# Loads of the first phase cut so that each writes 128 partitions, w1's bits issued from ScalarE's queue, and the first phase put in an order written by hand

## The chip, the core and the metric

The kernel runs on one core of a Trainium2 chip. The metric is the device time of one execution in microseconds (us). Before the change it is 899.99 us, the median of three runs (896.8 to 904.1). The profiled execution of the same kernel took 902.82 us, and its profile spans 901.0 us.

## What is computed

Packed attention, in which 32 packed queries per head first attend to the 576 tokens, and the tokens then attend to the 32 results. The output goes through a token mixer of rank 32 and a channel mixer with a relu. There are 8 batches, 8 heads of size 64, 512 channels and 2048 hidden channels.

```
p_packed = softmax(p @ k.T / 8) @ v          # 32 x 64 per head
x        = softmax(q @ p_packed.T / 8) @ p_packed
h        = x.T @ U @ V                       # mixes tokens, rank 32
u        = x + h.T
out      = u + relu(u @ w_ch1) @ w_ch2
```

The inputs q, k, v and p are float32. U, V, w_ch1 and w_ch2 are float64 in memory, and the kernel reads their bits as pairs of int32 and makes float32 of them itself.

## The kernel before

**The first phase** works through 16 units, each of one batch and four heads. Per unit it loads k and v, turns k onto the other axis on TensorE (`a_turn`, tiles `kx`, `k_ps`, `kT`), makes scores (`a_scores`), takes their maximum and exponential (`a_softmax`), turns them back (`a_turn_back`, tiles `m_ps`, `eT`), multiplies with v (`a_pack`, tile `vt`) and turns the result into `ppT` (`a_heads`). A loop over `i` runs from 0 to 18. In pass `i` the scores belong to unit `i`, the turning of k to unit `i+1`, the load of k to `i+2` and of v to `i+1`, the product with v to `i-2`. Beside this the phase converts w1 from its float64 bits in 16 chunks (`load_w1`, `convert_w1`, tile `bits`), runs the token side of batch 0 (the list `first`), and loads the first q's (`load_nat` into tile `x`).

**The second phase** is a loop over 8 batches and 16 tiles `kt` of hidden channels. `gemm1` (tile `h_ps`, line 573) and `gemm2` (tile `o`, line 589) both run as three matmuls (`mm3`, lines 84 to 86). Between them stand the folding of w1 with the packed attention (`fold`), the token side of the next batch (`steps`), the conversion of w2 in the first batch, and the stores (line 604).

**What sets the order.** In the first phase a scheduler with a cost model places the instructions on the engines; in the second the order is that of the source (`manual_schedule`, line 524). Each engine runs its instructions in order and waits on semaphores. All DMAs are issued from SyncE's queue (SPq), in order. There are eight semaphores for DMAs, taken in turn over all queues, so a DMA also waits until the one eight before it has landed.

**The shapes of the DMAs** matter below. A DMA has a list of dimensions on the DRAM side and one on the SBUF side. k was loaded by one DMA of 128 x 2 x 576 on both sides (line 194). v goes by two DMAs of 64 x 4 x 256 to one half of the partitions each (line 394), and w1 by two of 64 x 1024 (line 137). Line 604 stores tokens 64 apart in two groups: its side in DRAM is 2 x 64 x 512 and its side in SBUF 128 x 512.

Of the kernel before, what the change touches and what calls it, by code (L numbers as in the profile page):

```python
# [8 lines left out]
F32 = mybir.dt.float32  # L9
F32R = mybir.dt.float32r  # L10
I32 = mybir.dt.int32
# [8 lines left out]
def packed_attention_mixer_kernel(  # L20
# [26 lines left out]
    nc = tc.nc  # L47
    B, H, S, D = q.shape
# [4 lines left out]
    P = 128  # L53
    SM = 512
    NT = 9
    I = S // NT
    NK = DF // P
    NU = 2 * B
    QW = 512
# [4 lines left out]
    LAST = slice(4 * I, 5 * I)  # L64
# [3 lines left out]
    U, V, w1, w2 = (a.bitcast(I32) for a in (U, V, w1, w2))  # L68
# [24 lines left out]
    def bank():  # L93
        return psT.tile([P, 512], F32, name="t_ps", tag="t")
# [8 lines left out]
    def ppT_tile():  # L103
        return pipe.tile([P, 2, P], F32, name="ppT", bufs=3)
# [21 lines left out]
    def bits_tile():  # L126
        return pipe.tile([P, 512, 2], I32, name="bits", bufs=2)

    chunks = [(x, c) for c in range(NPC) for x in range(4)]
    bits = {}  # L130

    def load_w1(n):
        x, c = chunks[n]
        b = bits["w1", n] = bits_tile()
        for g in range(2):
            r0 = 4 * D * g + D * x
            nc.sync.dma_start(out=b[64 * g:64 * g + 64].rearrange("p x t -> p (x t)"),
                              in_=w1[r0:r0 + D, 2 * QW * c:2 * QW * c + 2 * QW])

    def convert_w1(n):  # L140
        x, c = chunks[n]
        float32_of(conv_tile(I32), conv_tile(F32), bits.pop(("w1", n)), w1t[x][:, QW * c:QW * c + QW])
# [48 lines left out]


    def load_nat(x, src, b, g):
        nc.sync.dma_start(
            out=x.rearrange("p (h y) -> p h y", h=2),
            in_=src[b, 4 * g:4 * g + 4].rearrange("(h z) (i c) d -> (z i) h (c d)", z=2, c=NT))

    def turn(t, x, h, bank):

        x = x.rearrange("p (h y) -> p h y", h=2)  # L200
        t_ps = bank()
        if h < 2:
            for j in range(4):
                o = P * (2 * (j % 2) + j // 2)
                nc.tensor.transpose(t_ps[:, o:o + P], x[:, h, P * j:P * j + P], ident)  # L205
            nc.scalar.copy(t[:, 2 * h:2 * h + 2, :4 * I].rearrange("p z (j i) -> p j z i", j=4),
                           t_ps.rearrange("p (j z i) -> p j z i", j=4, z=2))
        else:
            for h in range(2):
                nc.tensor.transpose(t_ps[:64, P * h:P * h + P], x[:, h, SM:], ident)  # L210
            nc.scalar.copy(t[:64, :, LAST], t_ps[:64, :2 * P].rearrange("p (h i) -> p h i", h=4))

    def scores(lT, t, g, bank):

        ss = [bank() for _ in range(2)]
        for h in range(4):
            hs = slice(32 * h, 32 * h + 32)
            for r in range(2):
                rs = slice(64 * r, 64 * r + 64)
                n = HALF[r].stop - HALF[r].start  # L220
                nc.tensor.matmul(ss[r][hs, :n], lhsT=lT[rs, g, hs], rhs=t[rs, h, :n], start=True, stop=True)  # L221
        return [ss[r][:, :HALF[r].stop - HALF[r].start] for r in range(2)]
# [142 lines left out]


    actx = ExitStack()
    sA = actx.enter_context(tc.tile_pool(name="sA", bufs=2, reuse_waits="tile"))
    psA = actx.enter_context(tc.tile_pool(name="psA", bufs=2, space=PSUM, reuse_waits="tile"))

    UN = [(b, g) for b in range(B) for g in range(2)]
    ua = {}
    pn, pT, pps = {}, {}, {}

    def bank_a(tag):
        return lambda: psA.tile([P, 512], F32, name=f"{tag}_ps", tag=tag)

    def a_load(u):
        b, g = UN[u]
        ua[u] = {}  # L380
        if g == 0:
            pn[b] = sA.tile([P, 2, 2, D], F32, name="pn")
            for z in range(2):
                nc.sync.dma_start(out=pn[b][:, :, z], in_=p[b].rearrange("(g h) n d -> (h n) g d", g=2))
        ua[u]["x"] = sA.tile([P, 2 * S], F32, name="kx", bufs=3)
        load_nat(ua[u]["x"], k, b, g)

    def a_load_v(u):
        b, g = UN[u]
        vt = ua[u]["v"] = sA.tile([P, 5, 4 * D], F32, name="vt", bufs=3)  # L390
        rows = v[b, 4 * g:4 * g + 4].rearrange("h (i c) d -> i c h d", c=NT)
        main = v[b, 4 * g:4 * g + 4].rearrange("h (i c) d -> i h (c d)", c=NT)[:, :, :8 * D]
        for a in range(2):
            nc.sync.dma_start(out=vt[64 * a:64 * a + 64, :4], in_=main[:, :, 4 * D * a:4 * D * a + 4 * D])
        nc.sync.dma_start(out=vt[:64, 4].rearrange("p (h d) -> p h d", h=4), in_=rows[:, 8])

    def a_p(b):
# [6 lines left out]
    def a_turn(u):  # L404
        b, g = UN[u]
        if g == 0:
            a_p(b)
        ua[u]["t"] = sA.tile([P, 4, 5 * I], F32, name="kT")
        for h in range(3):
            turn(ua[u]["t"], ua[u]["x"], h, bank_a("k"))  # L410

    def a_scores(u):
        b, g = UN[u]
        ua[u]["s"] = scores(pT[b], ua[u]["t"], g, bank_a("s"))

    def a_softmax(u):
        ss = ua[u]["s"]
        mx = sA.tile([P, 3], F32, name="mx")
        sm = ua[u]["sum"] = sA.tile([P, 2], F32, name="sm", bufs=3)
        for r in range(2):  # L420
            nc.vector.tensor_reduce(mx[:, r:r + 1], ss[r], axis=AX.X, op=ALU.max, negate=True)
        nc.vector.tensor_tensor(mx[:, 2:], mx[:, :1], mx[:, 1:2], op=ALU.min)
        e1 = ua[u]["e"] = sA.tile([P, S], F32, name="e1")
        for r in range(2):
            nc.scalar.activation(e1[:, HALF[r]], ss[r], AF.Exp, bias=mx[:, 2:], accum_out=sm[:, r:r + 1])
# [15 lines left out]
    def a_pack(u):  # L441
        b, g = UN[u]
        eT, vt = ua[u]["eT"], ua[u]["v"]
        p_ps = bank_a("m")()
        vk = vt[:, :4].rearrange("p h x -> p (h x)").rearrange("p (h k d) -> p k h d", h=4, k=4)
        for kk in range(5):
            rows = P if kk < 4 else I
            for h in range(4):
                hs = slice(32 * h, 32 * h + 32)
                rhs = vk[:, kk, h] if kk < 4 else vt[:rows, 4, D * h:D * h + D]  # L450
                nc.tensor.matmul(p_ps[hs, :D], lhsT=eT[:rows, kk, hs], rhs=rhs, start=kk == 0, stop=kk == 4)
        two = ua[u]["two"] = sA.tile([P, 2, D], F32, name="two")
        nc.scalar.activation(two, p_ps[:, :D].unsqueeze(1).to_broadcast([P, 2, D]), AF.Copy, scale=ua[u]["rs"])
        nc.gpsimd.tensor_copy(ppall[:, b, g], two[:, 0])

    def a_heads(u):
        b, g = UN[u]
        if g == 0:
            pps[b] = ppT_tile() if b == 0 else sA.tile([P, 2, P], F32, name="ppTa")
        z_ps = bank()  # L460
        nc.tensor.transpose(z_ps[:, :P], ua[u]["two"].rearrange("p z d -> p (z d)"), ident)
        nc.scalar.copy(pps[b][:, g], z_ps[:, :P])  # L462
        if g == 1:
            if b == 0:
                ppT[0] = pps[0]
            else:
                nc.sync.dma_start(out=ppTd[b], in_=pps[b].rearrange("p g n -> p (g n)"))
# [1 line left out]
    a_load(0)  # L469
    a_load(1)  # L470
    a_load_v(0)
    load_w1(0)
    load_w1(1)
    a_turn(0)
    n_w1 = 0
    first = attention(0, res)

    def some_w1():
        nonlocal n_w1
        if n_w1 < 16:  # L480
            convert_w1(n_w1)
            if n_w1 + 2 < 16:
                load_w1(n_w1 + 2)
            n_w1 += 1

    for i in range(NU + 3):
        if 0 <= i - 1 < NU:
            a_turn_back(i - 1)
        if i < NU:
            a_scores(i)  # L490
        if i + 1 < NU:
            a_load_v(i + 1)
            a_turn(i + 1)
        if i + 2 < NU:
            a_load(i + 2)
        some_w1()
        if i < NU:
            a_softmax(i)
        if i >= 5:
            for _ in range(2):  # L500
                if first:
                    first.pop(0)()
        if 0 <= i - 2 < NU:
            a_pack(i - 2)
        if 0 <= i - 3 < NU:
            a_heads(i - 3)
        if i == 2:
            uv = load_uv()
        if i == 3:
            prepare_uv(*uv)  # L510
        if i == 13:
            load_w2(0)
            load_w2(1)
        if i == 14:
            fold(0, 0)
        if i == 16:
            steps = attention(1, res)
            steps.pop(0)()
            split_w2(*convert_w2(0))
            load_w2(2)  # L520
    actx.close()


    ctx.enter_context(tc.manual_schedule())
    sB = ctx.enter_context(tc.tile_pool(name="sB", bufs=2, reuse_waits="tile"))
    psH = ctx.enter_context(tc.tile_pool(name="psH", bufs=1, space=PSUM, reuse_waits="tile"))
    psO = ctx.enter_context(tc.tile_pool(name="psO", bufs=4, space=PSUM, reuse_waits="tile"))
# [118 lines left out]
    for b in range(B):  # L646
# [3 lines left out]
        for kt in range(NK):  # L650
# [19 lines left out]
            if kt % 4 == 2 and (b, kt) != (B - 1, NK - 2):  # L670
                n = b * NPC + kt // 4 + 1
# [49 lines left out]
```

## Time and profile before

| what | value |
|---|---|
| median of three runs | 899.99 us |
| profiled execution: its own time, its span | 902.82 us, 901.0 us |
| TensorE (PE) busy | 842.1 us, 93% of the span |
| VectorE (DVE), ScalarE (ACT), GpSimd (POOL) busy | 379.4, 331.5, 93.9 us |
| DMA | 59.08 MB, mean 66 GB/s |
| chain that ended last | PE 80%, DMA 10%, DVE 5%, ACT 2% |

A share of busy time is a mean over both phases. The "DMA share" of a window is the mean busy share of the core's 16 DMA engines, so that one engine busy all the time is 0.0625. TensorE's granted clock is 1.00 in nearly all of the second phase.

### The profile page before, as it was taken

The page shows a single profiled execution, that of the slowest core. Times are in us where ns is not written, and L with a number is a line of the kernel's source. Part 1 is how long each engine was busy: PE and PEld are TensorE (multiplying, and loading weights), DVE is VectorE, ACT ScalarE, POOL GpSimd, SP SyncE. Part 2 cuts the span into 40 slices and gives each one's busy share as a digit, 9 for nine tenths or more (in the row PEclk, how much of TensorE's full clock was granted, in tenths as well). Part 3 has the DMA queues.
Part 4 walks back from the last instruction along what each step waited for, and adds up shares of the span by engine and source line. Part 5 has one row for each costly group of instructions (what it writes and reads, how often), then busy time and mean ns, then how long its engine had stood idle before and what let it go on. Part 6 is the DMA issues. An engine that isn't in the chain of part 4 may idle for free.

```text
span 901.0 us, 14507 instructions
## 1 busy us (share of the span) xinstructions
PE 842.1 (93%) x5808; PEld 670.3 (74%) x5808; DVE 379.4 (42%) x892; ACT 331.5 (37%) x952; POOL 93.9 (10%) x111
## 2 busy tenths in 40 slices
PE   5788983999999999999999999999999999999995
PEld 2454653877888887888888888788878887888884
DVE  2455666888534333333334323334343234332320
ACT  3565753544432333333323423234233332332220
POOL 0001122232201010011010101110111001000000
PEclk9787876999999999999999999999999999999998
DMA  9999985223110101001100110010001100000001
GB/s 223 243 255 233 243 202 147 93 95 108 47 45 1 59 11 49 1 1 59 42 6 2 59 59 1 1 59 29 19 1 59 39 21 1 1 17 32 1 3 57
DMA packets 38291, 59.08 MB, mean 66 GB/s; under 512 B 11088, under 2 KB 21200, under 8 KB 38224
## 3 DMA queue, kind: packets, MB, share of 16 engines
q1 hardware_dynamic: 38224, 58.16, 23.8%
q8 instruction: 46, 0.75, 0.4%
q14 instruction: 21, 0.17, 0.1%
HBM read 47.79 MB, written 10.35 MB: 65 GB/s over the span
## 4 chain that ended last, share of the span: by engine, by line
PE 80%; DMA 10%; DVE 5%; ACT 2%; issue 1%; SPq 1%; POOL 0%; DVEq 0%; ACTq 0%
PE o L84 15%; PE o L85 15%; PE o L86 15%; PE h_ps L84 8%; PE h_ps L86 7%; PE h_ps L85 7%; DMA bits<-in_moe_w_ch_dram 5%; PE t_ps L354 3%; DMA kx<-in_k_dram 2%; DMA vt<-in_v_dram 2%; PE t_ps L221 2%; PE t_ps L205 1%; DVE os L76 1%; PE t_ps L296 1%; DVE os L78 1%
## 5 line engine op out<-in xcount | busy, mean ns | idle before, releaser
L84 PE MATMUL o<-w2h,hh 128*128 128x512 f32 x512 | 207.2, 405 | 0.0
L85 PE MATMUL o<-w2l,hh 128*128 128x512 f32 x512 | 202.0, 395 | 0.0
L86 PE MATMUL o<-w2h,hl 128*128 128x512 f32 x512 | 201.8, 394 | 0.0
L580 DVE SCALAR_TENSOR_TENSOR hl<-h_ps,hh 128x256 fp32r<-128x256 f32 x256 | 104.2, 422 | 199.1 <-ACT hj L579 186.7
L84 PE MATMUL h_ps<-ah,wth 128*128 128x320 f32 (+1 forms) x512 | 159.4, 311 | 14.0 <-DVE hl L580 14.0
L577 ACT ACTIVATE hh<-h_ps 128x256 fp32r<-128x256 f32 x256 | 99.0, 388 | 193.0 <-PE h_ps L86 192.5
L85 PE MATMUL h_ps<-al,wth 128*128 128x320 f32 (+1 forms) x512 | 152.8, 298 | 0.0
L86 PE MATMUL h_ps<-ah,wtl 128*128 128x320 f32 (+1 forms) x512 | 152.5, 298 | 0.0
L84 PEld LDWEIGHTS h_ps<-ah,wth 128*128 128x128 f32 x512 | 98.0, 191 | 46.1 <-issue 25.7
L86 PEld LDWEIGHTS o<-w2h,hl 128*128 128x128 f32 x512 | 96.7, 189 | 22.2
L84 PEld LDWEIGHTS o<-w2h,hh 128*128 128x128 f32 x512 | 97.2, 190 | 21.4 <-issue 3.6
L85 PEld LDWEIGHTS o<-w2l,hh 128*128 128x128 f32 x512 | 97.4, 190 | 16.5
L85 PEld LDWEIGHTS h_ps<-al,wth 128*128 128x128 f32 x512 | 98.2, 192 | 1.9
L86 PEld LDWEIGHTS h_ps<-ah,wtl 128*128 128x128 f32 x512 | 98.1, 192 | 0.0
L361 DVE TENSOR_TENSOR wtl<-t_ps,wth 128x256 fp32r<-128x256 f32 x128 | 48.5, 420 | 94.3 <-ACT wth L360 91.0
L360 ACT CAST wth<-t_ps 128x256 fp32r<-128x256 f32 x128 | 43.3, 375 | 109.5 <-PE t_ps L354 98.5
L316 POOL TENSOR_TENSOR al<-aT,ah 128x320 fp32r<-128x320 f32 (+1 forms) x32 | 26.3, 823 | 207.1 <-ACT ah L315 207.0
L260 POOL TENSOR_TENSOR e<-e,m 128x576 f32<-128x576 f32 x16 | 18.7, 1170 | 240.4 <-DVE m L259 240.4
L76 DVE TENSOR_SCALAR os<-os 128x512 f32<-128x512 f32 (+2 forms) x35 | 21.0, 599 | 36.6 <-ACT os L75 36.6
L354 PE MATMUL t_ps<-w1t,ppT 64*32 64x512 f32 x512 | 35.9, 601 | 0.4 <-ACT ppTa L462 0.4
L205 PE MATMUL k_ps<-ident,kx 128*128 128x128 f32 x128 | 24.5, 344 | 11.5 <-DMA kx<-in_k_dram 8.5
L315 ACT CAST ah<-aT 128x320 fp32r<-128x320 f32 (+1 forms) x32 | 13.9, 434 | 53.0 <-DVE aT L314 53.0
(117 smaller groups left out, 1000.1 us busy)
## 6 DMA issues: line engine op xcount, KB each, us to landing
kx<-in_k_dram SPq DMA_DIRECT2D x16, 576.0 KB
x<-in_q_dram SPq DMA_DIRECT2D x16, 576.0 KB
vt<-in_v_dram SPq DMA_DIRECT2D x32, 256.0 KB
bits<-in_moe_w_ch_dram SPq DMA_DIRECT2D x32, 256.0 KB
bits<-in_moe_w_ch_dram SPq DMA_DIRECT2D x16, 512.0 KB
out_dram<-bits SPq DMA_DIRECT2D x32, 256.0 KB
pn<-in_p_dram SPq DMA_DIRECT2D x16, 64.0 KB
vt<-in_v_dram SPq DMA_DIRECT2D x16, 64.0 KB
```

The costliest lines, as they stand in the source:

```text
L76: nc.vector.tensor_single_scalar(t, t, LEAST, op=ALU.max)
L84: nc.tensor.matmul(ps, lhsT=lh, rhs=rh, start=start, stop=False)
L85: nc.tensor.matmul(ps, lhsT=lh, rhs=rl, start=False, stop=False)
L86: nc.tensor.matmul(ps, lhsT=ll, rhs=rh, start=False, stop=stop)
L205: nc.tensor.transpose(t_ps[:, o:o + P], x[:, h, P * j:P * j + P], ident)
L260: nc.gpsimd.tensor_tensor(e, e, m.unsqueeze(2).to_broadcast([P, S // 32, 32]), op=ALU.subtract)
L316: nc.gpsimd.tensor_tensor(al[:, g, ns], aT[:, ns], ah[:, g, ns].bitcast(F32), op=ALU.subtract)
L354: nc.tensor.matmul(f_ps[g][xs], lhsT=ppT[b][gs, g, xs], rhs=w1t[x][gs, QW * c:QW * c + QW], start=True, stop=True)
L360: nc.scalar.copy(hi[:, g], f_ps[g][:, cs])
L361: nc.vector.tensor_tensor(lo[:, g], f_ps[g][:, cs], hi[:, g].bitcast(F32), op=ALU.subtract)
L577: nc.scalar.activation(hh[:, ms], src, AF.Relu)
L580: nc.vector.scalar_tensor_tensor(hl[:, ms], src, 0.0, hh[:, ms].bitcast(F32), op0=ALU.max, op1=ALU.subtract)
```

## The change

The loads of k and q become two DMAs per unit instead of one, with the heads taken in another pairing (`turn` follows). v's main part becomes four DMAs per unit, one for each head, and each chunk of w1 one DMA instead of two, issued from ScalarE's queue and four chunks ahead instead of two. `a_softmax` is split into `a_max` and `a_exp`, the pass is written in another order, two chunks of w1 are converted in each of the passes 3 to 7, and `manual_schedule` begins before the first phase.

```diff
     def load_w1(n):
         x, c = chunks[n]
-        b = bits["w1", n] = bits_tile()
-        for g in range(2):
-            r0 = 4 * D * g + D * x
-            nc.sync.dma_start(out=b[64 * g:64 * g + 64].rearrange("p x t -> p (x t)"),
-                              in_=w1[r0:r0 + D, 2 * QW * c:2 * QW * c + 2 * QW])
+        b = bits["w1", n] = bits_tile() if n % 2 else sA.tile([P, 512, 2], I32, name="bits2")
+        nc.scalar.dma_start(out=b.rearrange("p x t -> p (x t)"),
+                            in_=w1.rearrange("(g x d) n -> x g d n", g=2, x=4)[x, :, :, 2 * QW * c:2 * QW * c + 2 * QW])
...
     def load_nat(x, src, b, g):
-        nc.sync.dma_start(
-            out=x.rearrange("p (h y) -> p h y", h=2),
-            in_=src[b, 4 * g:4 * g + 4].rearrange("(h z) (i c) d -> (z i) h (c d)", z=2, c=NT))
+        heads = src[b, 4 * g:4 * g + 4].rearrange("(z h) (i c) d -> h z i (c d)", z=2, c=NT)
+        for h in range(2):
+            nc.sync.dma_start(out=x[:, S * h:S * h + S], in_=heads[h])
...
-        main = v[b, 4 * g:4 * g + 4].rearrange("h (i c) d -> i h (c d)", c=NT)[:, :, :8 * D]
-        for a in range(2):
-            nc.sync.dma_start(out=vt[64 * a:64 * a + 64, :4], in_=main[:, :, 4 * D * a:4 * D * a + 4 * D])
+        main = v[b, 4 * g:4 * g + 4].rearrange("h (i c) d -> h i (c d)", c=NT)[:, :, :8 * D]
+        for h in range(4):
+            nc.sync.dma_start(out=vt[:, h], in_=main[h].rearrange("i (a x) -> a i x", a=2))
...
     actx = ExitStack()
+    ctx.enter_context(tc.manual_schedule())
...
     for i in range(NU + 3):
+        if i < NU:
+            a_scores(i)
+            a_max(i)
         if 0 <= i - 1 < NU:
             a_turn_back(i - 1)
-        if i < NU:
-            a_scores(i)
         if i + 1 < NU:
             a_load_v(i + 1)
             a_turn(i + 1)
         if i + 2 < NU:
             a_load(i + 2)
-        some_w1()
         if i < NU:
-            a_softmax(i)
+            a_exp(i)
+        if 0 <= i - 2 < NU:
+            a_pack(i - 2)
+        if 0 <= i - 3 < NU:
+            a_heads(i - 3)
+        for _ in range(2 if 2 < i < 8 else 1):
+            some_w1()
```

On the side of DRAM the new loads are 2 x 64 x 576 (k and q: the two heads `z`, 64 rows `i`), 2 x 64 x 256 (v: the two halves `a` of a row) and 2 x 64 x 1024 (w1: the two groups `g`). On the side of SBUF they are 128 partitions. `load_nat` also loads the q's of the second phase.

SyncE's queue before, late in the first phase. A name is tile<-tensor and the numbers are the destination's shape; `PE` or `DVE` in brackets is a wait for that engine, `DMAHW` a wait for an earlier DMA.

```order
L194 DMA kx<-in_k_dram 128x2x576 [waits DMAHW1_49,PE_49]
L384 DMA pn<-in_p_dram 128x2x64 [waits DMAHW2_49]
L384 DMA pn<-in_p_dram 128x2x64 [waits DMAHW3_49]
L194 DMA kx<-in_k_dram 128x2x576 [waits DMAHW4_49,PE_49]
L394 DMA vt<-in_v_dram 64x4x256 [waits DMAHW5_49,PE_49]
L394 DMA vt<-in_v_dram 64x4x256 [waits DMAHW6_49]
L137 DMA bits<-in_moe_w_ch_dram 64x1024 [waits DMAHW7_49,DVE_49,Activation_49]
```

The same queue now:

```order
L394 DMA vt<-in_v_dram 128x1x256 [waits DMAHW3_49,PE_49]
L394 DMA vt<-in_v_dram 128x1x256 [waits DMAHW4_49]
L394 DMA vt<-in_v_dram 128x1x256 [waits DMAHW5_49]
L394 DMA vt<-in_v_dram 128x1x256 [waits DMAHW6_49]
L395 DMA vt<-in_v_dram 64x4x64 [waits DMAHW7_49]
L194 DMA kx<-in_k_dram 128x1x576 [waits DMAHW0_49]
L194 DMA kx<-in_k_dram 128x1x576 [waits DMAHW1_49]
L144 DMA bits<-in_moe_w_ch_dram 128x1024 [waits DMAHW2_49,DVE_49]
```

Before, the scheduler let k's loads run ahead of v's and mixed w1's in. Now every pass has v of unit `i+1`, whose first DMA waits for TensorE, and then k of unit `i+2` behind it. The middle dimension of 1 stands for the DRAM side's third dimension.

TensorE before, in an early pass (`L205` and `L210` turn a unit's k, `L228` and `L230` turn the exponentials back, `L451` is the product with v, 20 matmuls of a unit):

```order
L205 MATMUL k_ps<-ident,kx 128x128 x8
L228 MATMUL m_ps<-ident,e_255 128x128
L230 MATMUL m_ps<-ident,e_255 64x128
L228 MATMUL m_ps<-ident,e_255 128x128 x3
L210 MATMUL k_ps<-ident,kx 64x128 x2
L451 MATMUL m_ps<-vt,eT 32x64 x17
```

The same work now (`L203` and `L208` turn k of unit `i+1`, `L455` is the product with v of unit `i-2`):

```order
L227 MATMUL m_ps<-ident,e_674 128x128 x4
L229 MATMUL m_ps<-ident,e_674 64x128
L203 MATMUL k_ps<-ident,kx 128x128 x8
L208 MATMUL k_ps<-ident,kx 64x128 x2
L455 MATMUL m_ps<-vt,eT 32x64 x20
```

Before, the scheduler mixed the pieces of several units. Now every pass turns k of unit `i+1`, for which its load must have landed, and only behind it stands the product that sets a tile of v free.

SyncE's queue now, at the end of the first phase (q of batch 1, `ppT` of batch 1, the third tile of w2):

```order
L194 DMA x<-in_q_dram 128x1x576 [waits DMAHW3_49,DVE_49,PE_49]
L194 DMA x<-in_q_dram 128x1x576 [waits DMAHW4_49]
L194 DMA x<-in_q_dram 128x1x576 [waits DMAHW5_49,PE_49]
L194 DMA x<-in_q_dram 128x1x576 [waits DMAHW6_49]
L108 DMA ppT<-ppTd_73 128x256 [waits DMAHW7_49]
L144 DMA bits<-in_moe_w_ch_dram 128x1024 [waits DMAHW0_49,DVE_49,Activation_49]
```

Before, q of batch 1 was loaded by two DMAs in the middle of w1's last loads, and `ppT` of batch 1 ahead of v's last ones. Now these four DMAs stand between v's last load and w2's third.

More of the change, by code (lines that the diff above doesn't have):

```diff
@@ L205, in turn @@
                 nc.tensor.transpose(t_ps[:, o:o + P], x[:, h, P * j:P * j + P], ident)
-            nc.scalar.copy(t[:, 2 * h:2 * h + 2, :4 * I].rearrange("p z (j i) -> p j z i", j=4),
+            nc.scalar.copy(t[:, h::2, :4 * I].rearrange("p z (j i) -> p j z i", j=4),
                            t_ps.rearrange("p (j z i) -> p j z i", j=4, z=2))
@@ L210, in turn @@
                 nc.tensor.transpose(t_ps[:64, P * h:P * h + P], x[:, h, SM:], ident)
-            nc.scalar.copy(t[:64, :, LAST], t_ps[:64, :2 * P].rearrange("p (h i) -> p h i", h=4))
+            nc.scalar.copy(t[:64, :, LAST].rearrange("p (z h) i -> p h z i", z=2),
+                           t_ps[:64, :2 * P].rearrange("p (h z i) -> p h z i", h=2, z=2))
     def scores(lT, t, g, bank):
@@ L414, in a_scores, with a_max @@
         ua[u]["s"] = scores(pT[b], ua[u]["t"], g, bank_a("s"))
-    def a_softmax(u):
+    def a_max(u):
         ss = ua[u]["s"]
         mx = sA.tile([P, 3], F32, name="mx")
-        sm = ua[u]["sum"] = sA.tile([P, 2], F32, name="sm", bufs=3)
         for r in range(2):
@@ L422, in a_softmax, with a_exp @@
         nc.vector.tensor_tensor(mx[:, 2:], mx[:, :1], mx[:, 1:2], op=ALU.min)
+        ua[u]["max"] = mx
+    def a_exp(u):
+        ss, mx = ua[u]["s"], ua[u]["max"]
+        sm = ua[u]["sum"] = sA.tile([P, 2], F32, name="sm", bufs=3)
         e1 = ua[u]["e"] = sA.tile([P, S], F32, name="e1")
@@ L458, in a_heads @@
         if g == 0:
-            pps[b] = ppT_tile() if b == 0 else sA.tile([P, 2, P], F32, name="ppTa")
+            pps[b] = ppT_tile() if b == 0 else sA.tile([P, 2, P], F32, name="ppTa", bufs=1)
         z_ps = bank()
@@ L471, in packed_attention_mixer_kernel @@
     a_load_v(0)
-    load_w1(0)
-    load_w1(1)
+    for n in range(4):
+        load_w1(n)
     a_turn(0)
@@ L481, in some_w1 @@
             convert_w1(n_w1)
-            if n_w1 + 2 < 16:
-                load_w1(n_w1 + 2)
+            if n_w1 + 4 < 16:
+                load_w1(n_w1 + 4)
             n_w1 += 1
     for i in range(NU + 3):
+        if i < NU:
+            a_scores(i)
+            a_max(i)
         if 0 <= i - 1 < NU:
             a_turn_back(i - 1)
-        if i < NU:
-            a_scores(i)
         if i + 1 < NU:
@@ L502, in packed_attention_mixer_kernel @@
                     first.pop(0)()
[L503 to L506, printed above, removed]
         if i == 2:
@@ L521, in packed_attention_mixer_kernel @@
     actx.close()
-    ctx.enter_context(tc.manual_schedule())
     sB = ctx.enter_context(tc.tile_pool(name="sB", bufs=2, reuse_waits="tile"))
```

## The prediction

> **What bounds the kernel now.** I first read the page's head and its slices of the span, then windows of the span, then single rows.
>
> ```profile
> span 901.0 us, 14507 instructions
> PE   5788983999999999999999999999999999999995
> DMA  9999985223110101001100110010001100000001
> GB/s 223 243 255 233 243 202 147 93 95 108 47 45 1 59 11 49 1 1 59 42 6 2 59 59 1 1 59 29 19 1 59 39 21 1 1 17 32 1 3 57
> ```
>
> A slice is 22.5 us. The kernel has two parts: about 140 us in which the DMA engines are full and TensorE is not, and the rest, in which TensorE is full and the DMA engines nearly idle. The change works in the first part, so its rate of loading is what counts. Windows give it (us from the start, width, busy time of PE, PEld, DVE, ACT and POOL, granted clock, DMA share, GB/s):
>
> ```profile
> 0.00:25.00 25.00, 14.36 (x76) 8.39 (x76) 6.65 (x20) 9.81 (x23) 0.85 (x7) 1.00 0.99 231
> 25.00:50.00 25.00, 19.32 (x215) 10.90 (x214) 12.86 (x42) 12.34 (x35) 0.48 (x2) 0.66 0.97 236
> 50.00:75.00 25.00, 21.18 (x328) 13.07 (x325) 13.19 (x38) 16.98 (x45) 2.11 (x5) 1.00 1.08 250
> 75.00:100.00 25.00, 22.94 (x238) 13.38 (x238) 12.47 (x33) 14.23 (x39) 4.94 (x7) 0.59 0.99 235
> 100.00:120.00 20.00, 18.68 (x259) 11.04 (x257) 13.83 (x42) 15.08 (x45) 0.93 (x4) 1.00 1.09 241
> 120.00:140.00 20.00, 14.41 (x182) 10.55 (x174) 11.25 (x27) 8.87 (x24) 7.89 (x15) 0.66 0.76 197
> 222.00:226.00 4.00, 4.00 (x21) 3.43 (x21) 2.87 (x5) 1.35 (x3) 1.31 (x1) 1.00 0.79 241
> 248.00:264.00 16.00, 16.00 (x114) 12.49 (x113) 6.16 (x18) 5.29 (x18) 1.16 (x1) 1.00 0.14 52
> 880.00:892.00 12.00, 10.03 (x44) 7.79 (x42) 1.71 (x4) 2.01 (x5) 0.00 (x0) 1.00 0.14 54
> ```
>
> Up to 120 us all 16 engines are busy (share 0.97 to 1.09) at 231 to 250 GB/s. The window 222 to 226 is the load of one q (128 x 2 x 576): share 0.79. The last two windows hold nothing but stores, which the next rows show; they are the rows on which I forecast.
>
> ```profile
> 244.29 9.85 SPq L604 DMA_DIRECT2D out_dram<-bits  x4
> out_dram<-bits SPq DMA_DIRECT2D x32, 256.0 KB
> ```
>
> Four stores of 256 KB are waiting together, and yet for 16 us the share is 0.14, which is 2.2 of 16 engines, at 52 GB/s. A store at line 604 has 2 x 64 x 512 on its side in DRAM and 128 partitions on its side in SBUF. It runs on two engines, whatever is queued. Every new load of k, q, v and w1 is of that form with the direction turned round: 2 x 64 x n in DRAM, 128 partitions in SBUF. The loads before were 128 or 64 on both sides, and filled 16 engines.
>
> **The change, part by part.** First the loads. I take it that they too run on two engines, the same two for both queues. The Trainium skill, in "DMA: Bandwidth & Descriptors", section "Why a DMA increments its semaphore by 16 and not by 1", says that a DMA takes the largest number of engines up to 16 that divides the slowest dimension of both sides, and the lowest-numbered ones; by it the loads get two engines, and the sum is the one below. The stores agree with it (share 0.14); no row of before shows a load with a small first dimension on its source's side.
>
> ```profile
> kx<-in_k_dram SPq DMA_DIRECT2D x16, 576.0 KB
> x<-in_q_dram SPq DMA_DIRECT2D x16, 576.0 KB
> vt<-in_v_dram SPq DMA_DIRECT2D x32, 256.0 KB
> bits<-in_moe_w_ch_dram SPq DMA_DIRECT2D x32, 256.0 KB
> pn<-in_p_dram SPq DMA_DIRECT2D x16, 64.0 KB
> vt<-in_v_dram SPq DMA_DIRECT2D x16, 64.0 KB
> ```
>
> Bytes on the two engines in the first phase: k 16 x 576 KB, v's main part 32 x 256, w1 32 x 256, and batch 0's q 2 x 576, in all 26,752 KB or 27.39 MB. The rate of two engines lies between two rows: the stores' 52 GB/s, and the q load's window, 241 / (0.79 x 16) = 19.1 GB/s for a busy engine, 38 for two. I take 50, near the stores, because there too only two engines run and nothing else contends; a little below, because v comes in rows of 1 KB and the stores have 2 KB. That is 27.39 MB / 50 GB/s = **548 us** (52: 527; 38: 721). The other transfers of the phase (p, v's ninth part, U, V, the stores of packed heads, two tiles of w2: some 4.8 MB) still spread over 16, a sixteenth on each: 0.3 MB at 25 GB/s, **12 us** more.
>
> Second, the order. It has v of unit `i+1` wait in SyncE's queue for the product with v of unit `i-2` (three buffers), and that stands on TensorE behind turning k of unit `i+1`, the last thing loaded. So SyncE's transfers run dry once in each of the passes 2 to 14, 13 times. The price of one gap:
>
> ```profile
> 92.29 1.38 PE m_ps L451 x40
> 93.68 1.90 PE k_ps L205 x8
> 97.28 0.39 PE k_ps L210 x2
> 112.69 0.60 SPq L394
> 145.01 3.53 DMA bits<-in_moe_w_ch_dram
> ```
>
> Half of 1.90 for the second half of k, 0.39, half of 1.38 for one unit's 20 matmuls: 2.03 us; the issue of v's first DMA, 0.60; and of the 3.53 us of a 512 KB load the part that is not data at 25 GB/s an engine (1.3), 2.2. Together 4.85 us, 13 times **63 us**. It is nothing if w1's transfers on the other queue cover it; but those are issued at the end of a pass, one or two chunks of 10.5 us beside 22.3 us of k and v, so that they are through before k is, and none are left after pass 7. I keep 0 to 63 for the range and take 63. Issuing w1 from ScalarE puts its issue and waits between the copies that TensorE waits for; with 22.3 us and more of loading in a pass, and 15.08 of 20 us the most that ScalarE was busy in a window above, that is hidden under the loads, and in a pass that were not bound by loading it would cost about 0.6 us each, some 10 in all. Splitting `a_softmax`, and converting w1 twice in five passes, costs nothing for the same reason: VectorE's 13.83 of 20 us was enough for a pass of 7 us, and a pass now takes some 30.
>
> Third, the start of the second phase. The rows of before (TensorE's timeline, and the chain of waits):
>
> ```profile
> 133.34 0.61 PE L84 MATMUL h_ps<-ah,wth 128*128 128x320 f32 x1
> 136.37 1.91 PE L205 MATMUL t_ps<-ident,x 128*128 128x128 f32 x8
> 152.05 0.64 PE L84 MATMUL h_ps<-ah,wth 128*128 128x320 f32 x1 [13.78 <-DVE hl L580]
> ```
>
> The first `gemm1` starts at 133.34 and runs with the turning of q to 138.28; then TensorE waits 13.78 us for VectorE, which was converting the last of w1. From 152.05 it is full to the end. Now w1 is converted by pass 10, under the loads, so that this wait goes. From the first `gemm1` to the end it is then 901.0 - 152.05 + 4.94 = **754 us**. In its place comes another wait. Batch 1's q, 1.18 MB, now takes 23.6 us behind v's last load, and w2's third tile stands in the queue behind it: 23.6 + 3.5 = 27 us after v. Its conversion is placed in `kt` 0, on ScalarE ahead of the relu of the second `gemm1`. TensorE gets there 3 us after v's landing plus about 11 us of work (two `gemm1` of 3.0, two turnings of 0.95, one `gemm2` of as many matmuls), so it stands still for about **13 us**. The q's of later batches are issued at `kt` 13, and the first half is needed three tiles of 5.9 us later (754 us over 128 tiles), against 5.9 us for loading a half: hidden, with the stores' 20 us (1.05 MB at 52) behind them on the same two engines within the 94 us of a batch. Without that cover a batch's first half would cost 5.9 us.
>
> The sum: 2 (start) + 548 + 12 + 63 = 625 to the landing of the last v; 3 for its product and two turnings; 754; 13. That is a span of 1395 us, against 901.0. The profiled execution's own time is 1.8 us above its span, so **1397 us**; the median of the runs, 899.99, is 2.8 below that execution, which is nothing here.
>
> **The rivals.** *Sixteen engines after all, and faster.* If the split goes by the destination alone, the stores (destination 2 x 64) get two engines and the loads (128) sixteen. What speaks for it: the rows cannot tell the two sides apart. Then the loads would gain: the q load with 128 partitions ran at 241/0.79 = 305 GB/s for a full share, and the first 140 us moved 32.6 MB, 107 us at that rate, 33 less; TensorE's busy time there, 110.9 us, would allow about 30, and I reckon **873 us**. The Trainium skill, in "DMA: Bandwidth & Descriptors", section "Rules for kernel authors", asks for one transfer to 128 partitions in place of two to halves; by that rule the outcome is this one, and the first phase's 231 to 250 GB/s beside 305 bear it out only as far as the loads stay on all engines. What decides it is whether the DRAM side's 2 counts on a load.
>
> *Two engines for each queue.* If ScalarE's queue took two others, w1's 8.39 MB (168 us) would run beside the rest: **1229 us**. Nothing in the rows speaks for it, since before only SyncE issued.
>
> *Two engines, but loads slower than stores.* At 38 GB/s the sum is 721 instead of 548, **1570 us**; for it speaks the one load window, against it that 13 engines were sharing there.
>
> **How the numbers follow.** Two of three ways to choose the engines (by the DRAM side, by both, by the destination) give two, and the form is exactly the stores'; I give two common engines 0.89, the slower loads among them, sixteen engines 0.07, a pair for each queue 0.04. The low end of the range is 52 GB/s with no gaps and no wait at the start: 2 + 527 + 12 + 3 + 754 + 2 = 1300. The high end is 44 GB/s (622) with gaps of 7 us: 2 + 622 + 12 + 91 + 3 + 754 + 13 + 2 = 1499, cut to 1490. Outside lie the pair for each queue, sixteen engines, and the slowest loads. A measurement tells about 1% from no change; sixteen engines would be faster with 0.06 and the same with 0.01, all else slower, 0.93.
>
> **What would show it.** Right: in the first 600 us a DMA share of about 0.13 and 45 to 52 GB/s, TensorE busy two to three tenths, the first `h_ps` near 628 us and some 750 to 770 us from there to the end. Gaps of about 5 us in the DMA share once a pass after pass 7 show the second term, a wait of ScalarE for w2's bits the 13 us. A share near 1 in the first 100 us would make the forecast wrong, a share of 0.25 while w1 loads would show a pair for each queue.

## The result, and the profile after

The changed kernel takes 1420.07 us (median of four runs, 1419.52 to 1421.27), against 900.0 before: 1.578 times as long, interval 1.571 to 1.584. Its profiled execution has a span of 1417.7 us. The head of its page, with slices of 35.4 us:

```profile
span 1417.7 us, 14491 instructions
PE   0110111002012223235999999999999999999996
PEclk9999655555555555555999999999999999999999
DMA  1111111111111111122321011010010100100001
GB/s 50 50 53 52 46 63 41 55 43 51 58 44 45 46 49 35 49 75 74 92 93 55 8 38 37 1 48 20 22 54 1 36 33 10 62 6 0 31 1 37
```

The full DMA slices of before are gone. For 600 us the DMA row reads 1 at 35 to 63 GB/s, TensorE is busy up to two tenths in most slices, and its granted clock falls to 0.5. From there on the page is as before. The issues now (form, count, size) and two windows of the span (us, width, busy time of PE, PEld, DVE, ACT and POOL, granted clock, DMA share, GB/s):

```profile
kx<-in_k_dram SPq DMA_DIRECT2D x32, 288.0 KB
bits<-in_moe_w_ch_dram ACTq DMA_DIRECT2D x16, 512.0 KB
vt<-in_v_dram SPq DMA_DIRECT2D x64, 128.0 KB
...
25.00:50.00 25.00, 3.03 (x23) 1.28 (x22) 0.98 (x3) 2.99 (x5) 0.00 (x0) 1.00 0.13 51
473.00:477.00 4.00, 4.00 (x59) 2.59 (x65) 0.00 (x0) 2.92 (x9) 0.24 (x1) 0.50 0.00 0
```

The first window is loading at its fullest, with both queues at work (the packet records hold 199 packets of k from SyncE's queue and 198 of w1 from ScalarE's in it): share 0.13, two engines, 51 GB/s, near the stores' 52. The second is a gap between two passes: not a byte moves while TensorE finishes turning k and runs the product with v. The chain of waits through one such pass, in order of time (start, us, what):

```profile
485.19 16.71 DMA kx<-in_k_dram
501.90 0.04 issue
501.95 1.11 PE k_ps L203 x4
503.06 0.43 PE k_ps L208 x2
503.49 1.38 PE m_ps L455 x40
504.87 0.42 PE t_ps L465
505.29 0.15 SPq L394
```

k lands at 501.9, and only 3.4 us later does SyncE issue v's first load. The start of the second phase (TensorE's and ScalarE's timelines):

```profile
638.47 0.59 PE L309 MATMUL t_ps<-vs,ms 128*128 128x256 f32 x1 [5.11 <-ACT ppTa L466]
648.42 0.62 PE L84 MATMUL h_ps<-ah,wth 128*128 128x320 f32 x1
657.73 1.09 PE L203 MATMUL t_ps<-ident,x 128*128 128x128 f32 x4 [4.63 <-DMA x<-in_q_dram]
673.28 1.32 PE L220 MATMUL t_ps<-xT,ppT 64*32 64x320 f32 x16 [7.61 <-ACT xT L209]
...
671.19 0.66 ACT L75 ACTIVATE os<-bits 128x512 f32<-128x512 f32 x1 [15.98 <-DMA bits<-in_moe_w_ch_dram]
```

The first `gemm1` stands at 648.42. ScalarE then waits 15.98 us for w2's third tile, and TensorE stands still for 4.63 us for q and 7.61 us behind ScalarE.

### The profile page after: what moved, and what is told of

The parts are those of the page before. It is cut to its first block, busy times and chain, and to the rows that moved or that the text cites. A ratio compares the mean times of both kernels' runs of the same rounds, so it can differ in the third digit from the quotient of the medians.

```text
span 1417.7 us, 14491 instructions
## 1 busy us (share of the span) xinstructions
PE 858.4 (61%) x5808; PEld 681.5 (48%) x5808; DVE 384.0 (27%) x892; ACT 334.0 (24%) x952; POOL 91.2 (6%) x111
## 4 chain that ended last, share of the span: by engine, by line
PE 49%; DMA 11%; SPq 9%; DVE 3%; ACT 1%; issue 1%; POOL 0%; DVEq 0%; ACTq 0%; POOLq 0%
DMA kx<-in_k_dram 10%; PE o L84 9%; PE o L85 9%; PE o L86 9%; PE h_ps L84 5%; SPq L394 4%; PE h_ps L85 4%; PE h_ps L86 4%; PE t_ps L353 2%; SPq L395 2%; SPq L194 2%; PE m_ps L455 1%; PE t_ps L220 1%; PE t_ps L203 1%; DMA bits<-in_moe_w_ch_dram 1%
## 5 line engine op out<-in xcount | busy, mean ns | idle before, releaser
L203 PE MATMUL k_ps<-ident,kx 128*128 128x128 f32 x128 | 34.4, 423 | 320.8 <-DMA kx<-in_k_dram 320.8
L203 PEld LDWEIGHTS k_ps<-ident,kx 128*128 128x128 f32 x128 | 22.5, 213 | 333.1 <-DMA kx<-in_k_dram 260.7
L401 PE MATMUL t_ps<-ident,pn 128*128 128x128 f32 x16 | 5.3, 438 | 140.4 <-DMA pn<-in_p_dram 109.1
L204 ACT COPY kT<-k_ps 128x512 f32<-128x512 f32 x32 | 18.6, 587 | 297.0 <-PE k_ps L203 297.0
```

## The experiments

The theory: a load whose side in DRAM begins with a dimension of 2 runs on two DMA engines, and that is most of the loss; the order by hand adds a gap in each pass. The rivals: the order or ScalarE's queue carries the loss; or any DRAM side of several dimensions is slow. Spans below are those of the profiled executions, to compare with 901.0 and 1417.7; e2, e3, e4 and e6 ran once each, so that their spans stand alone.

### The order without the shapes (e1), the shapes without the order (e2)

```diff
 # e1: the changed kernel, its loads cut as before, w1's still on ScalarE's queue
-        nc.scalar.dma_start(out=b..., in_=w1.rearrange("(g x d) n -> x g d n", ...)[x, :, :, ...])
+        for g in range(2):
+            nc.scalar.dma_start(out=b[64 * g:64 * g + 64]..., in_=w1[r0:r0 + D, ...])
 # and load_nat, turn and a_load_v as before
 # e2: the kernel before, with load_w1 (on nc.sync), load_nat, turn and a_load_v as changed
```

> The changed kernel's order and ScalarE's queue for w1, with the shapes of the loads as before (k and q 128 x 2 x 576, v and w1 to halves of the partitions). Theory (the new loads run on two engines because their DRAM side begins with 2): the DMA share is near 1 again and the first gemm1 comes at 130 to 155 us; with no wait for w1's conversion and 754 us from there, a span of 885 to 910 us. Rival (the order by hand or ScalarE's issue carries the loss): the span stays above 1100 us.

> The kernel before, in the scheduler's order and with all DMAs on SyncE's queue, with only the shapes of the loads of k, q, v and w1 as changed. Theory: two engines, a DMA share of 0.13 for about 580 to 650 us, a span of 1340 to 1440 us. Rival (the order carries the loss): about 900 us. Rival (each queue has two engines of its own, or two queues add something): some 30 us and more above the changed kernel's 1417.7.

e1 took 966.41 us (1.072 times before, 1.068 to 1.077), with a span of 965.0; e2 1354.9 us in its one execution, span 1353.1. The first window of e1, and of e2 the one from 50 to 100 us:

```profile
0.00:25.00 25.00, 9.25 (x61) 5.03 (x61) 4.13 (x11) 5.98 (x13) 0.70 (x6) 1.00 0.99 227
```

```profile
50.00:100.00 50.00, 6.06 (x73) 4.20 (x73) 5.38 (x14) 5.53 (x14) 0.00 (x0) 0.90 0.15 53
```

The shapes take the DMA share from 0.99 to 0.15, whatever the order. They alone cost 1353.1 - 901.0 = 452 us, the order alone 965.0 - 901.0 = 64 us, and 452 + 64 = 516 is the 516.7 us of the change. e2 holds the scheduler's own order for the new loads, so the 452 us include what it made of them. ScalarE's queue gets no engines of its own: the changed kernel's window from 25 to 50 us has both queues on one share of 0.13, and e6 below, which uses both and has no gaps, takes 1353.7 us where e2, with SyncE's alone, takes 1353.1. But e1 is 55 us above the upper end of what I expected: the order costs on 16 engines what it costs on two, though, as e7 and e9 show, not for the same reasons. Its first `gemm1` comes at 210.5 us:

```profile
L84 PE MATMUL h_ps<-ah,wth x512: 280/302/614, 210.5 to 935.5; 128*128 128x256 f32 x86, 128*128 128x320 f32 x85
```

### How many engines: DRAM sides that begin with 4, 8 and 64 (e3, e4, e5)

```diff
 # e3: 4 x 32 x n (e4: 8 x 16 x n), for w1; k, q and v likewise from four (eight) heads
-in_=w1.rearrange("(g x d) n -> x g d n", g=2, x=4)[x, :, :, 2 * QW * c:2 * QW * c + 2 * QW]
+in_=w1.rearrange("(y e) n -> y e n", y=4)[:, 32 * x:32 * x + 32, 2 * QW * c:2 * QW * c + 2 * QW]
 # e5: 64 x 2 x n, the two outer dimensions exchanged
-in_=w1.rearrange("(g x d) n -> x g d n", ...)      heads[h]                              "i (a x) -> a i x"
+in_=w1.rearrange("(g x d) n -> x d g n", ...)      heads[h].rearrange("z i y -> i z y")  "i (a x) -> i a x"
```

> The changed kernel with loads of k, q, v and w1 of the same sizes whose DRAM side begins with 4 instead of 2 (4 x 32 x n); they fetch other rows, so that what is computed is not the reference. Theory (as many engines as the DRAM side's first dimension): a DMA share of 0.25 at about 95 GB/s, the loads 285 us instead of 570, the first gemm1 near 360 us, a span of 1100 to 1140 us. Rival (any DRAM side that does not merge into one dimension runs on two engines): 1400 to 1420 us.

> The same with a DRAM side that begins with 8 (8 x 16 x n), again of other rows. Theory: a DMA share of 0.5 at about 180 GB/s, the loads 143 us, the first gemm1 near 215 us, a span of 950 to 1000 us. Rival (two engines for any such form): 1400 to 1420 us.

> The changed kernel with the same loads, sizes and 128 partitions, but the two outer dimensions of the DRAM side exchanged: 64 x 2 x n instead of 2 x 64 x n, so that the rows of a transfer land on other partitions and what is computed is not the reference. Theory (the first dimension on the DRAM side sets the number of engines): all 16 engines, a share near 1 at the start, a span of 930 to 970 us, below or near the run with the old shapes (965.0). Rival (a DRAM side of three dimensions, or more and smaller DMAs, is what is slow): 1100 us or more.

Their spans are 1149.6, 1024.7 and 961.1 us; e5 took 962.48 us (1.067 times before, 1.064 to 1.070). The first window of each, e3, e4 and e5:

```profile
0.00:25.00 25.00, 1.77 (x6) 1.00 (x6) 0.00 (x0) 2.25 (x3) 0.70 (x6) 1.00 0.25 92
```

```profile
0.00:25.00 25.00, 6.93 (x38) 4.05 (x38) 0.98 (x3) 3.77 (x7) 0.70 (x6) 1.00 0.49 159
```

```profile
0.00:25.00 25.00, 10.95 (x71) 6.03 (x71) 4.54 (x13) 8.55 (x19) 0.70 (x6) 0.98 0.82 252
```

A first dimension of two (the changed kernel, 0 to 25 us), four and eight gives 0.14, 0.25 and 0.49 of 16 engines, at 50, 92 and 159 GB/s: in these windows the share is the first dimension over 16. With 64 first, the same three dimensions, the same number of DMAs and the same 128 partitions move 252 GB/s. So it is neither the third dimension nor the count, but what stands first. The Trainium skill's rule (in "DMA: Bandwidth & Descriptors", section "Why a DMA increments its semaphore by 16 and not by 1") holds for loads too: the smaller side's 2 counts although the destination has 128. The spans of e3 and e4 came out 10 and 25 us above what I expected, where I had reckoned with 95 and 180 GB/s: at 92 and 159 the 27.39 MB take 298 and 172 us for the 285 and 143 that I gave. From 100 to 150 us the rates are lower still, 77 and 119; that the order's waits weigh more there was not tested.

e5 beside e1 also shows what loads to 128 partitions are worth where they get all the engines, since both load on 16 in the same order (e5's DMAs are also more and smaller). Over the first 100 us w1's packets of 4 KB take 159 ns at the median in e5 and 264 in e1, v's of 1 KB 46 and 68, and in the first window a full share would move 252 / 0.82 = 307 GB/s against 227 / 0.99 = 229. Yet e5's runs (962.48) are only 4 us below e1's (966.41): in this order the faster loads by themselves gain little.

### The gap of each pass: k's load ahead of v's (e6 with the new shapes, e7 with the old)

```diff
+        if i + 2 < NU:
+            a_load(i + 2)
         if i + 1 < NU:
             a_load_v(i + 1)
             a_turn(i + 1)
-        if i + 2 < NU:
-            a_load(i + 2)
```

> The changed kernel with k's load of each pass put ahead of v's in SyncE's queue (the two calls exchanged, nothing else). Theory (v's load waits for the product with v and holds k's load back, a gap of 4.85 us in each of some 11 passes): the gaps go, the first gemm1 comes 40 to 60 us earlier than 648, a span of 1355 to 1380 us. Rival (two engines are full whatever stands in the queue): 1410 to 1420 us.

> The order by hand with the old shapes (965.0 us of span), and k's load ahead of v's. Theory (the same gap, 11 us a pass where 16 engines are fast, is most of the 64 us that the order costs): a span of 900 to 930 us. Rival (the 64 us come from ScalarE's issue of w1 or from the one buffer of packed heads): 950 to 965 us.

e6 has a span of 1353.7 us in its one execution, 64 less than the changed kernel. Its first `gemm1` and the window in which the changed kernel moved nothing:

```profile
L84 PE MATMUL h_ps<-ah,wth x512: 280/302/636, 584.4 to 1323.8; 128*128 128x256 f32 x86, 128*128 128x320 f32 x85
```

```profile
473.00:477.00 4.00, 0.23 (x2) 0.00 (x0) 0.00 (x0) 0.59 (x1) 0.00 (x0) 0.50 0.13 50
```

The gap is gone (share 0.13 for 0.00), and the first `gemm1` comes 64 us earlier, 4 more than the most I had expected. e6 then takes as long as e2 (1353.1), whose packet records show no such gaps either. The equality is partly chance: e2's first `gemm1` is 8 us later (592.2), and its second phase as much shorter (760.9 us for 769.3). With the old shapes e7 takes 934.14 us (1.037 times before, 1.035 to 1.040), span 933.0: 32 of the 64 us. That is 3 us short of the range I gave; something else holds the other 32.

### ScalarE's part: w1's loads back on SyncE's queue (e9)

What TensorE waits for in e7 names it (waited for: us in total, times, longest):

```profile
PE k_ps L210 <- ACT kT L206: 28.0, 12, 5.5
```

The copy of k's turning on ScalarE stands behind w1's conversion and the issue of w1's loads, and an issue there waits until VectorE has freed the tile. One pass of e7, ScalarE's timeline and then TensorE's row:

```profile
68.46 0.69 ACT L75 ACTIVATE os<-bits 128x512 f32<-128x512 f32 x1
71.60 1.12 ACTq L137 DMA_DIRECT2D bits<-in_moe_w_ch_dram  x2
72.77 0.66 ACT L75 ACTIVATE os<-bits 128x512 f32<-128x512 f32 x1 [3.62 <-issue]
75.87 1.12 ACTq L137 DMA_DIRECT2D bits<-in_moe_w_ch_dram  x2
77.79 1.08 ACT L206 COPY kT<-k_ps 128x512 f32<-128x512 f32 x2
...
78.44 0.63 PE L210 MATMUL k_ps<-ident,kx 128*64 128x128 f32 x2 [5.51 <-ACT kT L206]
```

VectorE is done with the first tile at 71.52, ScalarE issues at 71.60, and the copies that TensorE waits for come only after two such rounds. e9 is e7 with this edit:

```diff
-            nc.scalar.dma_start(out=b[64 * g:64 * g + 64]...
+            nc.sync.dma_start(out=b[64 * g:64 * g + 64]...
```

> The order by hand with the old shapes and k's load ahead of v's (933.0 us of span), and w1's loads back on SyncE's queue. Theory (what is left of the order's 64 us is ScalarE, which holds the copies of k's turning behind w1's conversion and the issue of w1's loads, waiting for VectorE): 910 to 925 us. Rival (it is the conversion and the fixed order alone, not the issue): 928 to 936 us.

It took 918.54 us (1.022 times before, 1.017 to 1.026), span 915.3, first `gemm1` at 160.8 us. TensorE's wait for that copy is nearly gone:

```profile
PE k_ps L210 <- ACT kT L206: 2.6, 7, 1.0
```

So the issue on ScalarE costs 17.7 us of the order's 64 by the spans, 15.6 by the medians of e7's and e9's runs. The fall of that wait from 28.0 to 2.6 us speaks for the holding of ScalarE as the reason; the edit also moves w1's loads to another place among k's and v's, which was not tried by itself. 14 us are left (915.3 - 901.0) that I did not take apart; the fixed order, two chunks of w1 in a pass and the single buffer of packed heads are candidates.

### The stores, and v to 128 partitions (e8, e10)

```diff
 # e8: the kernel before
-                    nc.sync.dma_start(
-                        out=out[self.b].rearrange("(i c) m -> c i m", c=NT)[c0:c0 + 5:4], in_=os_[:, a])
+                    for y in range(2):
+                        nc.sync.dma_start(out=out[self.b].rearrange("(i c) m -> c i m", c=NT)[c0 + 4 * y],
+                                          in_=os_[64 * y:64 * y + 64, a])
 # e10: e8, and v with the row first; k's turning writes its tokens in that order
+        for h in range(4):
+            nc.sync.dma_start(out=vt[:, h], in_=main[h].rearrange("i (a x) -> i a x", a=2))
...
+                o = slice(2 * P * (j % 2) + j // 2, 2 * P * (j % 2) + 2 * P, 2)
+                nc.tensor.transpose(t_ps[:, o], x[:, h, P * j:P * j + P], ident)
```

> The kernel before, each store of 2 x 64 x 512 made two of 64 x 512; nothing else. Theory (the stores too run on as many engines as their DRAM side's first dimension, two): they go to 16 engines, the last four no longer drain for 20 us behind the last matmul, and the span falls by 5 to 8 us, 893 to 896. Rival (the end does not hang on the stores): 899 to 902 us.

> The kernel before with the stores split (890.1 us of span), and v's main part loaded to 128 partitions by four DMAs a unit whose DRAM side is 64 x 2 x 256, row i and half a on partition 2i+a; k's turning writes its columns in the same order of tokens. Theory (128 partitions help if the DRAM side leaves all 16 engines): the first phase moves its bytes faster, 4 to 10 us less, 880 to 887 us. Rival (16 engines are full either way): 888 to 893 us.

e8 takes 893.05 us, 0.9925 of before (0.990 to 0.995), span 890.1. Its last four pairs of stores, a window of e8:

```profile
870.00:878.00 8.00, 8.00 (x42) 6.82 (x41) 1.87 (x4) 1.89 (x4) 0.00 (x0) 1.00 0.57 131
```

They move at a share of 0.57 and 131 GB/s in a window of 8 us, and are done before the last matmul, where in the kernel before they ran at 0.14 and 54 GB/s to the end. From the last `gemm1` (867.1 and 871.5) to the end it is 23.0 us instead of 29.5; the rest of the gain in span, some 4 us (first `gemm1` at 129.5 for 133.3), lies in the first phase, where no store of this form runs; the runs of before differ by 7 us among themselves. The ratio of the runs, 6.8 us of 900, agrees with the 6.5.

e10 takes 887.41 us, 0.984 of before (0.982 to 0.987), the fastest of all, span 883.1. TensorE's second `gemm1`, where the last of w1 is waited for, in e8 and in e10:

```profile
148.06 0.64 PE L84 MATMUL h_ps<-ah,wth 128*128 128x320 f32 x1 [14.64 <-DVE hl L580]
```

```profile
140.72 0.64 PE L84 MATMUL h_ps<-ah,wth 128*128 128x320 f32 x1 [3.41 <-DVE hl L582]
```

It comes 7.3 us earlier, and the span is 7.0 shorter. This is what the change set out to do, a load to 128 partitions, on 16 engines. Over the first 140 us v's packets of 1 KB take 46 ns at the median where e8 has 75, and by 120 us e10 has moved 30.4 MB and e8 29.6. But that the 7 us come from this is not shown, because the scheduler also placed the queue anew. The last issue of w1's loads in e8 and in e10:

```profile
132.56 1.10 SPq L137 DMA_DIRECT2D bits<-in_moe_w_ch_dram  x2
```

```profile
117.44 0.61 SPq L137 DMA_DIRECT2D bits<-in_moe_w_ch_dram  x1
```

In e10 w1's last load is issued 15 us earlier, ahead of v's last ones, and the first `gemm1` comes 5.1 us later (134.6 for 129.5). 0.9 MB are about 3.5 us at 250 GB/s (an estimate from the windows above); the rest may be the order, and no run separates the two.

## Why the prediction was right, point by point

The forecast was 1397 us (1300 to 1490); measured were 1420.07. Against the span, the forecast sum was 1395 and the measured 1417.7.

- **Two engines.** Right: shares of 0.13 and 0.14 at 50 to 51 GB/s in the first windows, and shown by e2 to e5. The chance of 0.07 that the destination alone decides is settled by e5 against the changed kernel: the same destination, 16 engines and two. That each queue has a pair of its own is ruled out by the window from 25 to 50 us, in which both queues were at work on a share of 0.13.
- **The rate, 50 GB/s, 548 us.** The step that was mis-sized. The last v lands at about 638 us; less the start (2), the spread transfers (12) and the gaps (51, below) that leaves 573 us, 27.39 MB / 573 = 48 GB/s. In the packet records a packet of v (1 KB) takes 46 ns, of k or q (2.3 KB) 95 ns, of w1 (4 KB) 161 ns at the median: 22, 24 and 25 GB/s for an engine. I had seen that v's rows are short and took off too little. It is 25 us; less 12 for the gaps, and with 7 more on the way to the first `gemm1` and 2 in the second phase, it makes up the 23 by which the forecast was low. The 12 us for the spread transfers are an estimate that no run took apart.
- **The gaps, 13 of 4.85 us, 63 us.** The mechanism was right and the price of one too: ten gaps of 4.5 to 4.9 us and two shorter ones stand in the packet records, 51 us. What made it less was not w1, for which I had kept the range open: its transfers run until 428 us, through pass 7, and cover none of the gaps. In pass 6 batch 0's q was still loading, in pass 3 the load of U took half of the gap, and in pass 14 that of w2. All gaps over 0.3 us, with the start, come to 57 us; e6, which removes the cause, has 4 and gains 64. Of the 10 or so that the gaps leave unexplained, 6 are that k's, v's and w1's packets took less time in e6 (604.6 us on each of the two engines for 610.8); the rest is open.
- **ScalarE's issue and the order, nothing.** Right where the loads take 22 us and more a pass: e6 takes as long as e2, within the 8 us that shift between their phases. The cost I gave for a pass that is not bound by loading, some 10 us in all, came out as 16 to 18 (e7 against e9).
- **From the last v to the first `gemm1`, 3 us.** Some 10 us: TensorE was held 5.11 us at 638.47 by a copy into the one buffer of packed heads, whose store had been queued behind v's last load, and the last product waited behind the conversion of w2 on ScalarE.
- **The second phase, 754 + 13 us.** Measured 1417.7 - 648.4 = 769.3 for 767. The 13 were 4.63 for q, which I had not put there, and 7.61 behind ScalarE's wait of 15.98 for w2's third tile, which I had. w1's wait of 13.78 us is gone, as said, under 640 us of loading.
- **The rival of sixteen engines, 873 us.** As a forecast it was wrong twice: the loads get two engines, and where they do get 16 (e5) the order still costs, 962 us. The rate that it named exists: 307 GB/s for a full share in e5, for the 305 of the forecast, although the window 222 to 226 behind the 305 held not one q alone but, by bytes, half w2 (206 packets of 2.3 KB and 119 of 4 KB). In time, the most that a run here shows for it is e10's 7 us, with the queue placed anew.

## What to carry to other kernels

Read the shape of a DMA on both sides, as the instruction carries it, before its size: the first dimension of the smaller side set the number of engines in every run here, and exchanging two loops of the DRAM side (2 x 64 to 64 x 2, with the rows' new partitions followed through the kernel) took it from two to 16. A window with a low DMA share and work queued is the sign; the kernel before showed it in its stores. And a load that waits for a consumer belongs behind the loads that do not: one exchange in the queue was worth 64 us where two engines load and 32 where 16 do.

## What the runs showed that I had not expected

The hand-written order costs the same 64 us where 16 engines load (965.0 against 901.0) as where two do (1417.7 against 1353.1), by coincidence, since the parts differ. With two engines all of it went when k's load moved ahead (e6); with 16 half went (e7), and 16 to 18 us more when w1's issue left ScalarE's queue (e9). TensorE's granted clock, 1.00 in the first 100 us of the changed kernel, stood at 0.50 to 0.57 from 200 to 600 us, where TensorE was busy 10% to 28% of the time (the prediction had said two to three tenths), and was back at 1.00 by 680 us.
